# A fused attention, soft mixture of experts and feed-forward kernel: where tiles live, when weights are loaded, and dummy matmuls in the first units

## The chip, the cores and the metric

The kernel runs on one core of a Trainium2 chip. The metric is the time of one execution on the device in microseconds, as the median of some runs. A profile of one execution, taken by the hardware profiler, shows every instruction of the five engines: TensorE (PE; its weight loads are PEld), VectorE (DVE), ScalarE (ACT), GpSimd (POOL) and SyncE (SP), which here only issues transfers (DMAs).

## The reference

Three layers follow each other; all arrays are in float32, but `w_in` and `w_out` of the last layer come as 64-bit floats.

```python
# 1: attention with decay; B, H, S, D = 4, 8, 768, 48
for t in range(S):
    cur = einsum('bhd,bhe->bhde', u[None] * k_t, v_t)
    y[:, :, t] = einsum('bhd,bhde->bhe', r_t, state + cur)
    state = w[None, :, :, None] * state + einsum('bhd,bhe->bhde', k_t, v_t)
x = y.transpose(0, 2, 1, 3).reshape(3072, 384)
# 2: soft mixture of experts: 8 experts with 4 slots each
logits = x @ phi                                # 3072 x 32
slot_input = softmax(logits, over tokens).T @ x
slot_out[e] = relu(slot_input[e] @ w1[e]) @ w2[e]   # 384 -> 1024 -> 384
x = softmax(logits, over slots) @ slot_out
# 3: feed-forward
r = relu(x @ w_in); out = (r * r) @ w_out       # 384 -> 2048 -> 384
```

## The kernel before

The order of all work is written out by hand: each engine runs its instructions in the order of the code, and the framework only adds the waits. Transfers are issued by SyncE in the order of the code too, so a load that waits for its room holds up those behind it.

**Attention** goes in 16 units (`n`), four for each of the four batches; a unit is one batch and two heads, cut into six chunks of 128 tokens, in two groups of three. Each unit's inputs (r and k transposed in `tr`, and k, r and v in `krv`) are loaded into one of four unit slots; unit n+4 is loaded once unit n has been used. The steps of a unit, with their engines: `bonus` (GpSimd, two multiplications of the `krv` part, lines 237 and 238), `weigh` (VectorE, L242), `keys` (GpSimd, L248), `decay` (VectorE, L232, for k and for r), `diag` (GpSimd, L254, one for each group), `A` (TensorE, L264), `strict` (VectorE, L270, copies A's result onto diag's tile and so frees A's two banks), `KV` (TensorE, L278), `scan` (VectorE, L283, with a copy on ScalarE, L285), `Y` (TensorE, L301 and L307), `X` (L320, transposes the result into the tile of tokens xn) and `L` (L335, the logits). The loop at L440 interleaves units n-1, n and n+1; in it, `bonus(n+2)` is called at the end of turn n, `weigh(n+1)` and `keys(n+1)` at the start of turn n, and `KV(n+1)` in its middle. Two tiles xn take turns, for even and odd batches. `keep_clock(m)` issues m dummy matmuls of 128x256 on TensorE (L225), each of two instructions, into a bank that nobody reads. Before the first unit there are six.

**Weights.** `load_weight(i)` loads the next of 16 pieces of 1536 KB: the eight `w1[e]`, then the eight `w2[e]`. Nine have slots of their own and are loaded in the loop, one in each of the turns 0, 2, 3, 5, 6, 8, 9, 10 and 11, behind that turn's unit loads. The next three go into unit slots 0, 1 and 3 when their last units are done (turns 12, 13 and 15), and `load_win(0)` into unit slot 2. Two more (post0, post1) go where attention's tiles lay; that pool is closed as a whole after the last batch's sum over tokens (`soft_sum`, L378), at L528. The last two go into slots of w1 pieces after `up(1)` and `up(2)`.

**Experts.** `up(e)` (L564) and `down(e)` (L582) are TensorE's; `turn` transposes between them. `load_wout(f)` loads 128 rows of w_out (three buffers), and `wout_f32`, `conv_win` turn the 64-bit words into float32 in three steps on VectorE (L127, L129, L131). `wout_high` and `wout_low` split a piece of w_out in two parts. Before, three loads of w_out stand behind `up(3)`, and the parts 1 to 3 of w_in behind `up(4)` to `up(6)`; the conversions of w_out's pieces 0 to 2 and of w_in's parts 4 and 5 stand between the `down`s. Then follow `cstack` (L596, four transposes of the softmax over slots, with a copy on ScalarE, L597), the copy `so` of the outputs (L664), their transpose (L668, L671), and `G` (L677) with its split on ScalarE and VectorE (L681, L682).

**Feed-forward.** 96 turns in a loop (L774), each with one matmul of `s_h` (L725) and nine of the second product (L817) on TensorE; ScalarE and VectorE make relu, square and the split between them. In the turns 3, 11 and 19 `quarters` (L696) makes four more parts of G from w_in.

## Time and profile before

| | us |
|---|---|
| median of three runs (400.8 to 401.72) | 401.37 |
| the profiled execution, its own time | 400.18 |
| span of the profiled execution | 398.5 |
| TensorE busy in it | 381.7 |
| VectorE busy | 280.2 |
| ScalarE busy | 211.7 |
| GpSimd busy | 114.8 |

The transfers read 64.78 MB and write 4.72 MB. Attention lasts until about 129 us, the experts until about 158, the feed-forward loop from about 167 until the end.

How to read the rows: a stretch of the table of windows gives each engine's busy time in it with the number of instructions (x), the granted clock of TensorE as a share of 2.4 GHz, the mean share of the 16 transfer engines that was busy, and GB/s. A line of the timeline gives start, duration, engine, line of the kernel, operation, tiles (out<-in), and in brackets how long the engine was idle just before and what ended that. Instructions of the same kind that follow each other are one line (x); its duration reaches from the first start to the last end, and a matmul's end contains its drain. A busy TensorE is not TensorE at its peak.

### The profile page before, as it was taken

What the parts mean: (1) busy time and instruction counts of PE and PEld (TensorE: products, weight loads), DVE (VectorE), ACT (ScalarE), POOL (GpSimd) and SP (SyncE); (2) the same over time, 40 slices, a digit from 0 to 9 for tenths busy, and PEclk for the clock granted to TensorE, in tenths of its full rate; (3) what the DMA queues carried; (4) which work ended last, traced back from release to release, by engine and by line L of the source; (5) the groups of instructions that cost most, each with busy time, mean ns of one, the idle gap of its engine ahead of it and who ended that gap; (6) DMA issues with size and microseconds to landing.
All of it is one profiled execution on the core that took longest, in us unless ns stands there. A gap on an engine that the chain in (4) does not pass through costs nothing.

```text
span 398.5 us, 8194 instructions
## 1 busy us (share of the span) xinstructions
PE 381.7 (96%) x3219; PEld 294.2 (74%) x3219; DVE 280.2 (70%) x495; ACT 211.7 (53%) x465; POOL 114.8 (29%) x110
## 2 busy tenths in 40 slices
PE   5799999999999999789999999999999999999995
PEld 3677777767766564668787888888888888888884
DVE  5769897879974564799998567666566676566563
ACT  2224453453444451678888876555554564554552
POOL 3869997986870001122323120000000000000000
PEclk8559999999999999999999999999999999999999
DMA  7999999999995899913333202100000040000004
GB/s 245 344 320 343 389 407 403 404 404 406 405 383 188 307 410 405 375 47 102 85 100 87 63 0 104 56 0 2 0 0 2 0 159 2 0 0 2 0 0 158
DMA packets 25989, 70.81 MB, mean 178 GB/s; under 512 B 3680, under 2 KB 6112, under 8 KB 25952
## 3 DMA queue, kind: packets, MB, share of 16 engines
q1 hardware_dynamic: 25808, 70.10, 47.2%
q10 hardware_dynamic: 144, 0.20, 0.5%
q8 instruction: 25, 0.41, 0.4%
q14 instruction: 12, 0.10, 0.1%
HBM read 64.78 MB, written 4.72 MB: 174 GB/s over the span
## 4 chain that ended last, share of the span: by engine, by line
PE 80%; DMA 9%; DVE 6%; POOL 2%; issue 1%; ACT 1%; SPq 0%; POOLq 0%; ACTq 0%; DVEq 0%
PE ps_Y L817 16%; PE ps_A L817 16%; PE ps_kv L817 8%; PE ps_lg L817 8%; PE ps_A L264 7%; DMA wo<-in_w_out_dram 7%; PE ps_Y L307 5%; PE ps_Y L301 3%; PE ps_tr L320 3%; PE ps_tr L725 3%; PE ps_tab L725 3%; PE ps_lg L335 2%; DMA slot<-in_krv_dram 2%; PE ps_kv L278 2%; PE ps_tr L378 1%
## 5 line engine op out<-in xcount | busy, mean ns | idle before, releaser
L817 PE MATMUL ps_Y<-slot,slot 128*128 128x512 f32 x288 | 111.7, 395 | 0.0
L750 DVE TENSOR_TENSOR slot<-gg,slot 128x512 fp32r<-128x512 f32 (+1 forms) x97 | 66.5, 685 | 49.2 <-ACT slot L747 48.3
L817 PE MATMUL ps_A<-slot,slot 128*128 128x512 f32 x288 | 88.9, 393 | 0.6 <-DVE slot L682 0.6
L747 ACT CAST slot<-gg 128x512 fp32r<-128x512 f32 (+1 forms) x97 | 59.8, 618 | 50.5 <-DVE gg L744 49.9
L817 PEld LDWEIGHTS ps_A<-slot,slot 128*128 128x128 f32 x288 | 54.0, 188 | 13.2 <-DVE slot L682 1.0
L817 PEld LDWEIGHTS ps_Y<-slot,slot 128*128 128x128 f32 x288 | 54.1, 188 | 12.6 <-issue 0.6
L744 DVE TENSOR_TENSOR gg<-hr 128x512 f32<-128x512 f32 (+1 forms) x71 | 49.0, 691 | 14.3 <-ACT hr L737 14.2
L817 PE MATMUL ps_kv<-slot,slot 128*128 128x512 f32 x144 | 55.7, 394 | 0.0
L817 PE MATMUL ps_lg<-slot,slot 128*128 128x512 f32 x144 | 55.4, 391 | 0.0
L623 POOL TENSOR_TENSOR slot<-wf,slot 128x384 fp32r<-128x384 f32 x16 | 19.1, 1196 | 97.5 <-ACT slot L618 97.5
L270 DVE COPY_PREDICATED AT<-mask,ps_A 128x384 f32<-128x384 int32 x64 | 33.8, 583 | 9.2 <-PE ps_A L264 8.4
L264 PE MATMUL ps_A<-slot 48*128 48x128 f32 x384 | 36.2, 310 | 2.9 <-DVE slot L232 1.8
L264 PEld LDWEIGHTS ps_A<-slot 48*128 48x128 f32 x384 | 28.7, 204 | 10.3 <-DVE AT L270 3.6
L737 ACT ACTIVATE hr<-ps_tab 128x512 f32<-128x512 f32 x48 | 28.7, 599 | 12.9 <-PE ps_tab L725 12.9
L737 ACT ACTIVATE hr<-ps_tr 128x512 f32<-128x512 f32 (+1 forms) x49 | 28.8, 590 | 12.4 <-PE ps_tr L725 12.4
L313 ACT COPY xT<-ps_Y 112x256 f32<-112x256 f32 x64 | 17.4, 324 | 28.0 <-PE ps_Y L307 27.8
L254 POOL TENSOR_SCALAR_AFFINE_SELECT AT<-dg 128x768 f32<-128x768 f32 x32 | 28.0, 886 | 13.2 <-PE ps_Y L307 8.4
L817 PEld LDWEIGHTS ps_kv<-slot,slot 128*128 128x128 f32 x144 | 27.1, 188 | 6.2
L817 PEld LDWEIGHTS ps_lg<-slot,slot 128*128 128x128 f32 x144 | 27.0, 188 | 5.9
L232 DVE TENSOR_TENSOR slot<-slot,ps_tab 112x768 f32<-112x768 f32 x32 | 30.1, 941 | 0.6 <-DMA slot<-in_tr_dram 0.6
L307 PE MATMUL ps_Y<-AT,slot 128*48 128x128 f32 x384 | 29.6, 293 | 0.0
L307 PEld LDWEIGHTS ps_Y<-AT,slot 128*48 128x48 f32 x384 | 20.8, 129 | 6.5 <-issue 5.9
(168 smaller groups left out, 502.3 us busy)
## 6 DMA issues: line engine op xcount, KB each, us to landing
slot<-in_w_dram SPq DMA_DIRECT2D x14, 1536.0 KB, 11.1
slot<-in_tr_dram SPq DMA_DIRECT2D x32, 384.0 KB, 7.5
slot<-in_krv_dram SPq DMA_DIRECT2D x16, 448.0 KB, 7.3
slot<-in_krv_dram SPq DMA_DIRECT2D x16, 416.0 KB, 7.8
slot<-in_w_in_dram SPq DMA_DIRECT2D x4, 1536.0 KB, 19.1
wo<-in_w_out_dram SPq DMA_DIRECT2D x16, 384.0 KB, 3.3
out_dram<-os SPq DMA_DIRECT2D x15, 256.0 KB, 2.2
post<-in_w_dram SPq DMA_DIRECT2D x2, 1536.0 KB, 9.2
```

The source lines that it names most:

```text
L232: nc.vector.tensor_tensor(x, x, t.unsqueeze(1).to_broadcast([112, NC, 128]), ALU.mult)
L254: nc.gpsimd.affine_select(out=at.rearrange("p c h t -> p (c h) t"), in_=dg.rearrange("p c h -> p (c h)").unsqueeze(2).to_broadcast([128, 2 ...
L264: nc.tensor.matmul(p[h][:, i], tv[rows, 1, GC * g + i], tv[rows, 0, GC * g + i], start=True, stop=True)
L270: nc.vector.copy_predicated(at[:, :, h], mask.unsqueeze(1).to_broadcast([128, GC, 128]), p[h])
L307: nc.tensor.matmul(at_of(c, j), vv[:, c, h], at[:, c - GC * g, h], start=False, stop=True, skip_group_check=True)
L623: nc.gpsimd.tensor_tensor(wout_half(wls, f, WL), st.pop(("wf", f)), hi, ALU.subtract)
L725: nc.tensor.matmul(p, gst[:, 128 * f:128 * (f + 1)], cTall[:, 512 * g:512 * (g + 1)], start=True, stop=True)
L737: nc.scalar.activation(fs[i, "hr"][:, c], fs[i, "p"][:, c], AF.Relu)
L744: nc.vector.tensor_mul(gg, hr, hr)
L747: nc.scalar.copy(part(i, "gh")[:, c], fs[i, "gg"][:, c])
L750: nc.vector.tensor_tensor(part(i, "gl")[:, c], fs[i, "gg"][:, c], fs[i, "gh"].bitcast(F32)[:, c], ALU.subtract)
L817: nc.tensor.matmul(o, (hi, lo, hi)[k][:, 128 * j:128 * (j + 1)], (gh, gh, gl)[k], start=(f == 0 and k == 0), stop=(f == NF - 1 and k == 2))
```

## The change

1. Attention's short-lived tiles no longer lie in one pool. Three rooms (`yards`, `odd`, `even`) hold views of them: `yards` the three tiles of diag, the two of scan's copies and the table P; `odd` and `even` the two tiles xn, and `odd` also `pkn` and scan's result. Each room is given on as one, when all its views have been read: `even` to the three buffers of w_out's loads (after the third batch's sum), `yards` to the weight piece 12 (after the last Y), `odd` to the piece 13 (after the last sum). In the feed-forward loop the rings of `hr`, `gg` and `os` lie in `yards` and `odd`.
2. The first two weight pieces are loaded before the loop, ahead of unit 4; in the loop the turns 0, 2, 4, 6, 8, 10 and 11 load one.
3. Three loads of w_out are issued in turn 14; the parts 1 to 3 of w_in come behind all weights, two more w_out loads behind the first of them. Pieces 0 and 1 of w_out are converted ahead of the last batch's softmax, piece 2 at `down(3)`, and the parts 4 to 7 of w_in at `down(4)` to `down(7)`.
4. The outputs' copy `so` goes ahead of the first `cstack`; the third `cstack` goes into turn 16 of the loop.
5. 16 dummy matmuls instead of 6 before the first unit, and 14 more in groups of 4, 3, 3 and 4 around A, Y and KV of unit 0.

```diff
+    ROOM = {"yards": 3072, "odd": 3072, "even": 2310}
+
+    def room(tag, dt=F32):
+        cnt[0] += 1
+        return const.tile([128, ROOM[tag]], dt, name=f"{tag}{cnt[0]}", tag=tag, bufs=1)
...
     load_n(0)
+    yards, odd, even = (room(t) for t in ROOM)
+    att = att_cm.__enter__()
...
     def load_wout(f):
-        wst["o", f] = wk([128, DM, 2], "wo", NWO, I32, pool=mid)
+        if "wo" not in wst:
+            wst["wo"] = room("even", I32)
+        wst["o", f] = wst["wo"][:, 2 * DM * (f % NWO):2 * DM * (f % NWO + 1)].rearrange("p (d t) -> p d t", t=2)
...
-    home = list(range(NB, NSLOT)) + [0, 1, 3, "post0", "post1", NB + 1, NB + 2]
+    home = list(range(NB, NSLOT)) + [0, 1, 3, "yards", "odd", NB + 1, NB + 2]
...
-    SB = [att.tile([112, NC, D], F32, name=f"SB{i}") for i in range(2)]
-    pkn = att.tile([128, NP, 2, D], F32, name="pkn")
-    xn = [att.tile([128, NC, DM + 1], F32, name=f"xn{i}") for i in range(2)]
+    o = 3 * 2 * GC * 128
+    ATS = [yards[:, o // 3 * i:o // 3 * (i + 1)].rearrange("p (c h t) -> p c h t", c=GC, h=2) for i in range(3)]
+    SB = [yards[:112, o + NC * D * i:o + NC * D * (i + 1)].rearrange("p (c d) -> p c d", c=NC) for i in range(2)]
+    o = NC * (DM + 1)
+    xn = [x[:, :o].rearrange("p (c d) -> p c d", c=NC) for x in (even, odd)]
+    pkn = odd[:, o:o + DM].rearrange("p (a b d) -> p a b d", a=NP, b=2)
+    sc = odd[:112, o + DM:o + DM + D * NC].rearrange("p (d c) -> p d c", c=NC)
...
+        if i == 2 and 2 <= f < NF - NWO:
+            load_wout(f + NWO)
...
-    keep_clock(6)
+    keep_clock(16)
...
+    keep_clock(4)
     A(0, 0)
+    keep_clock(3)
...
-    nload = 0
+    for nload in range(2):
+        load_weight(nload)
+    nload = 2
     for n in range(NU):
...
+        if n == 0:
+            keep_clock(3)
         Y(n, 0)
+        if n == 0:
+            keep_clock(4)
...
-            if n not in (1, 4, 7):
+            if n not in (1, 3, 5, 7, 9):
                 load_weight(nload)
                 nload += 1
         elif n == NU - 2:
+            for f in range(NWO):
+                load_wout(f)
             load_win(0)
...
+    load_weight(nload)
+    nload += 1
 
     L(NU - 1, (1, 2))
     keep_clock(1)
+    for f in range(2):
+        for i in range(3):
+            wout_f32(f, i)
     soft_max(B - 1)
...
-    while str(home[nload]).startswith("post"):
-        load_weight(nload)
-        nload += 1
+    load_weight(nload)
+    nload += 1
...
-        if e == 3:
-            for f in range(NWO):
-                load_wout(f)
         if e in (4, 5, 6):
             load_win(e - 3)
+        if e == 4:
+            load_wout(NWO)
+            load_wout(NWO + 1)
...
-    hT = take(WIN[1])[:, :256 * E].rearrange("p (i e j f) -> p i e j f", i=E // 2, e=2, j=2)
+    hT = take(CT)[:, :256 * E].rearrange("p (i e j f) -> p i e j f", i=E // 2, e=2, j=2)
...
         down(e)
-        if e < 3:
+        if e in (1, 3):
+            wout_high(e // 2)
+            wout_low(e // 2)
+        if e == 3:
             for i in range(3):
-                wout_f32(e, i)
-            if e < 2:
-                wout_high(e)
-                wout_low(e)
-        elif e < 5:
-            conv_win(e + 1)
-    cstack(0, "lg")
+                wout_f32(2, i)
+        if e >= 4:
+            conv_win(e)
+    cTall = take(CT, F32R)
...
     nc.scalar.copy(so, acc[:, :DM])
+    cstack(0, "lg")
     cstack(1, "kv")
...
-    cstack(2, "lg")
     G(0, "A")
...
-    todo = [(f, i) for f in range(6, NF) for i in range(3)]
+    todo = [(f, i) for f in range(8, NF) for i in range(3)]
...
-        for _ in range(2 if i < 3 else 2 - half):
+        for _ in range(2 if i < 5 else 1):
...
-        if i in (22, 25, 28):
-            cstack(3 + (i - 20) // 3, ("tr", "tab")[(i + 1) % 2])
+        if i in (16, 22, 25, 28):
+            cstack(2 if i == 16 else 3 + (i - 20) // 3, ("tr", "tab")[(i + 1) % 2])
```

## Rows read from the trace of the kernel before

**Rows 1.** The page: busy tenths of TensorE and granted clock, in 40 slices of the span.

```profile
PE   5799999999999999789999999999999999999995
...
PEclk8559999999999999999999999999999999999999
```

**Rows 2.** Windows: stretch, length, five engines busy (PE, PEld, DVE, ACT, POOL), clock, DMA share, GB/s.

```profile
5.78:8.57 2.79, 0.00 (x1) 0.00 (x1) 2.51 (x14) 0.71 (x2) 0.06 (x1) 0.88 1.03 410
...
20.00:28.00 8.00, 8.00 (x69) 6.17 (x71) 5.22 (x8) 1.63 (x5) 5.46 (x5) 0.50 0.89 324
...
17.00:24.00 7.00, 6.56 (x68) 5.10 (x68) 5.74 (x9) 1.17 (x3) 6.77 (x7) 0.50 0.94 336
24.00:31.00 7.00, 7.00 (x92) 5.57 (x92) 3.33 (x7) 2.31 (x9) 3.95 (x5) 0.69 0.86 300
...
50.00:113.00 63.00, 62.16 (x998) 46.31 (x988) 54.38 (x93) 28.82 (x101) 53.52 (x46) 1.00 1.03 405
...
117.00:134.00 17.00, 15.87 (x200) 9.96 (x195) 6.80 (x20) 7.46 (x26) 0.81 (x1) 1.00 0.72 262
```

**Rows 3.** Timeline of the first units, TensorE and GpSimd.

```profile
1.43 4.36 PE L225 MATMUL ps_tr<-ident 128*128 128x256 f32 x12 [1.43 <-POOL ident masks.py:199]
...
4.97 0.81 PE L225 MATMUL ps_tr<-ident 128*128 128x256 f32 x3
...
11.33 1.65 PE L264 MATMUL ps_A<-slot 48*128 48x128 f32 x12 [1.75 <-DVE slot L232]
...
18.86 1.04 PE L278 MATMUL ps_kv<-slot 128*48 128x48 f32 x20 [0.44 <-POOL slot L248]
...
28.29 0.67 PE L278 MATMUL ps_kv<-slot 128*48 128x48 f32 x20
...
28.58 0.87 POOL L254 TENSOR_SCALAR_AFFINE_SELECT AT<-dg 128x768 f32<-128x768 f32 x1 [2.97 <-PE ps_Y L307]
```

**Rows 4.** Unit 3's last load: its issue (timeline), and its time to landing (DMA view).

```profile
16.59 0.43 SPq L92 DMA_DIRECT2D slot<-in_tr_dram  x1
...
slot<-in_tr_dram SPq DMA_DIRECT2D x1, 384.0 KB, 7.8
```

**Rows 5.** Timeline at units 4 and 5.

```profile
36.00 1.41 POOL L237 TENSOR_TENSOR slot<-slot,U 128x576 f32<-128x576 f32 x1
...
42.22 1.41 POOL L237 TENSOR_TENSOR slot<-slot,U 128x576 f32<-128x576 f32 x1
...
45.20 1.42 POOL L248 TENSOR_TENSOR slot<-slot,pkn 128x576 f32<-128x576 f32 x1
...
46.69 1.06 DVE L270 COPY_PREDICATED AT<-mask,ps_A 128x384 f32<-128x384 int32 x2
47.28 0.62 PE L278 MATMUL ps_kv<-slot 128*48 128x48 f32 x20
...
48.40 0.94 PE L264 MATMUL ps_A<-slot 48*128 48x128 f32 x12
```

**Rows 6.** Timeline at the last softmax over tokens.

```profile
129.30 0.42 DVE L343 TENSOR_REDUCE nmx<-ps_lg 96x1 f32<-96x256 f32 x1 [5.17 <-PE ps_lg L335]
```

**Rows 7.** Timeline from `down` to the first quarters.

```profile
154.28 0.36 DVE L127 TENSOR_SCALAR wf<-wo 128x384 int32<-128x384 int32 x1 [8.34 <-DMA wo<-in_w_out_dram]
...
154.67 0.56 DVE L129 SCALAR_TENSOR_TENSOR wf<-wo,wf 128x384 int32<-128x384 int32 x1
...
158.77 0.60 PE L596 MATMUL ps_kv<-ident,cs 128*128 128x128 f32 x4
...
159.99 0.94 PE L668 MATMUL ps_tr<-sel,so 128*128 128x128 f32 x6 [0.62 <-ACT so L664]
...
162.46 0.27 ACT L681 CAST slot<-ps_A 128x128 fp32r<-128x128 f32 x1 [0.48 <-PE ps_A L677]
...
163.24 0.29 DVE L682 TENSOR_TENSOR slot<-ps_A,slot 64x128 fp32r<-64x128 f32 x1
...
176.20 0.84 PE L696 MATMUL ps_tr<-slot,soT 128*32 128x128 f32 x18 [1.15 <-DVE slot L131]
```

More of the change, by code (lines that the diff above doesn't have):

```diff
@@ L163, in load_weight @@
         kind, e = W[i]
-        if str(home[i]).startswith("post"):
-            cnt[0] += 1
-            t = post.tile([128, 3072], F32, name=f"post_{cnt[0]}", tag=home[i], bufs=1)
-        else:
-            t = take(home[i])
+        t = (room if home[i] in ROOM else take)(home[i])
         if kind == "w1":
@@ L190, in rwkv_softmoe_ffn @@
     pw = att.tile([112, 2, 8], F32, name="pw")
-    P = att.tile([112, 2 * NP, 64], F32, name="P")
+    P = yards[:112, 2 * 2 * GC * 128:2 * 2 * GC * 128 + 2 * NP * 64].rearrange("p (a n) -> p a n", n=64)
     nc.vector.memset(P[:, :NP, 0:1], 1.0)
@@ L403, in slots_norm, with wout_half, wout_f32, wout_high @@
         nc.vector.tensor_mul(cnat[:, b], cnat[:, b], sm.unsqueeze(2).to_broadcast([128, NC, NS]))
+    whs, wls = {}, {}
+    def wout_half(half, f, homes):
+        if f // 8 not in half:
+            half[f // 8] = take(homes[f // 8], F32R).rearrange("p (c d) -> p c d", c=8)
+        return half[f // 8][:, f % 8]
+    def wout_f32(f, i):
+        if f >= NF:
+            return
+        if i == 0:
+            st["wf", f] = wk([128, DM], "wf", 2)
+        to_f32(st["wf", f], wst["o", f], (i,))
+        if i == 2 and 2 <= f < NF - NWO:
+            load_wout(f + NWO)
+    def wout_high(f):
+        if 0 <= f < NF:
+            nc.scalar.copy(wout_half(whs, f, WH), st["wf", f])
+    def wout_low(f):
+        if 0 <= f < NF:
+            hi = wout_half(whs, f, WH).bitcast(F32)
+            nc.gpsimd.tensor_tensor(wout_half(wls, f, WL), st.pop(("wf", f)), hi, ALU.subtract)
     P2 = const.tile([96, 2, DM + 1], F32, name="P2")
@@ L597, in cstack @@
         nc.scalar.copy(cTall[:, 512 * g:512 * (g + 1)], p)
-    whs, wls = {}, {}
-    def wout_half(half, f, homes):
-        if f // 8 not in half:
-            half[f // 8] = take(homes[f // 8], F32R).rearrange("p (c d) -> p c d", c=8)
-        return half[f // 8][:, f % 8]
-    def wout_f32(f, i):
-        if f >= NF:
-            return
-        if i == 0:
-            st["wf", f] = wk([128, DM], "wf", 2, pool=mid)
-        to_f32(st["wf", f], wst["o", f], (i,))
-        if i == 2 and f + NWO < NF:
-            load_wout(f + NWO)
-    def wout_high(f):
-        if 0 <= f < NF:
-            nc.scalar.copy(wout_half(whs, f, WH), st["wf", f])
-    def wout_low(f):
-        if 0 <= f < NF:
-            hi = wout_half(whs, f, WH).bitcast(F32)
-            nc.gpsimd.tensor_tensor(wout_half(wls, f, WL), st.pop(("wf", f)), hi, ALU.subtract)
     soft_turn(B - 1, slice(1, 2))
@@ L661, in rwkv_softmoe_ffn @@
     parts = take(PARTS, F32R).rearrange("p (i r c) -> p i r c", i=2, r=3)
+    yards, odd = room("yards"), room("odd")
+    rings = {"hr": [yards[:, 512 * i:512 * (i + 1)] for i in (0, 1)], "gg": [yards[:, 512 * i:512 * (i + 1)] for i in (2, 3)],
+             "os": [r[:, 512 * i:512 * (i + 1)] for r, i in ((yards, 4), (yards, 5), (odd, 0), (odd, 1))]}
+    nos = 0
     so = wk([128, DM], "so", 1, pool=ffn)
     nc.scalar.copy(so, acc[:, :DM])
+    cstack(0, "lg")
     cstack(1, "kv")
@@ L725, in s_h @@
         nc.tensor.matmul(p, gst[:, 128 * f:128 * (f + 1)], cTall[:, 512 * g:512 * (g + 1)], start=True, stop=True)
-        fs[i, "p"], fs[i, "hr"] = p, wk([128, 512], "hr", 2, pool=ffn)
-        fs[i, "gg"] = wk([128, 512], "gg", 2, pool=ffn)
+        fs[i, "p"], fs[i, "hr"], fs[i, "gg"] = p, rings["hr"][i % 2], rings["gg"][i % 2]
     def part(i, tag):
@@ L820, in rwkv_softmoe_ffn @@
                 tok = 512 * (2 * sg + half)
-                os = wk([128, 512], "os", 4, pool=ffn)
+                os = rings["os"][nos % 4]
+                nos += 1
                 for e in range(2):
```

5 lines of the change are left out of this document (1 added, 4 removed).

## The prediction

> **What bounds the kernel now.** I read the slices of the page first. TensorE is busy in tenths 9 from about 20 us to the end, in attention and in the feed-forward part alike, so the sum is one of TensorE's time: a microsecond counts only if it comes off TensorE's queue, a gap in it, or its clock [rows 1]. The slices show a granted clock of 0.5 (1.2 GHz, against 2.4) in three slices near the start, and the stretch 20 to 28 us in the table has 0.50 with TensorE busy all of it [rows 1, 2]. Six dummy matmuls ended near 5.8 us, TensorE then had nothing for 2.79 us while the decay tables were made, and the clock fell and stayed low through the real work of units 0 and 1 [rows 2, 3]. Second, the transfers: from 50 to 113 us they run at 405 GB/s with a share of 1.03, full; from 17 to 31 us at 300 to 336, and from 117 to 134 at a share of 0.72, so there is room early and late, but none between [rows 2]. Third, the gaps between the last `down` and the feed-forward loop, in the timeline [rows 7]. GpSimd is the engine to watch beside TensorE: a unit costs it two bonus steps, keys and two diags, 3 x 1.42 + 2 x 0.87 = 6.0 us, against 6.2 from one bonus to the next (36.00, 42.22) [rows 3, 5].
>
> **Dummy matmuls in the first units.** Ten more ahead of the decay tables, 14 more between the real steps of unit 0. Three dummy instructions at the high clock took 0.81 us including their drain; a dummy is two of them, so at most 0.54, and by their spacing 0.43 [rows 3]. Sixteen in a row end near 1.43 + 4.36 + 10 x 0.43 = 10.1 us, 1.5 past the start of the table transposes, which is hidden because the first A waits for VectorE until 11.33 [rows 3]. With the 4, 3, 3 and 4 more, and the real steps at about half their duration (KV 1.04 against 0.62, A 1.65 against 0.94), A(0,0) ends at 12.9, as before; KV(1) starts at 20.0, not at 18.86, where it waited for GpSimd; and KV(2) at 25.3 instead of 28.29 [rows 3, 5]. There GpSimd takes over: its diag that idled 2.97 us for TensorE until 28.58 no longer waits [rows 3]. So units 2 and 3 run **3.0 us** earlier, if their inputs are there.
>
> **Two weights before the loop.** This is where that gain goes. SyncE's loads share one queue, and the two weights are put between unit 3's loads and unit 4's. Unit 3's last load was issued at 16.59 and landed 7.8 later, at 24.4 [rows 4]. A weight is 384 x 1024 floats, 1.573 MB; a unit is 128 x (2 x 768 + 1728) floats, 1.671 MB. At 405 GB/s behind 24.4 us, two weights and unit 4 are 4.82 MB, 11.9 us, so unit 4 is in at 36.3 us; one more weight, which the loop issues behind it, and unit 5 make 8.0, so 44.3 [rows 2, 4]. Before, unit 4's bonus started at 36.00 and unit 5's at 42.22 [rows 5]. The slack behind a late bonus: keys(5) ended at 45.20 + 1.42 = 46.62 and TensorE's KV(5) began at 47.28, 0.66 us; and on VectorE weigh(5) and decay(5,1), which wait for unit 5, stand ahead of strict(4,1), which freed A's two banks at 47.75 for A(5,0) at 48.40, 0.65 us [rows 5]. So unit 4 lets attention be at most 0.4 earlier than before (36.3 - 36.00 - 0.7), whatever the clock does, and unit 5 makes it 44.3 - 42.22 - 0.65 = **1.4 us later**. From there TensorE has no gaps in which to make it up [rows 1]. Bounds: if the transfer engines' spare time between 17 and 24 us (69 GB/s under 405, 0.48 MB) takes the weights in early, 1.2 less, +0.2; if the 300 GB/s of 24 to 31 us holds although more is queued, 1.7 more, +3.1 [rows 2]. I take the middle, since the queue behind these loads is then as deep as at 50 us. Later units don't bind: every second unit of the loop brings no weight, and two units with one weight are 4.92 MB, 12.1 us, against 12.4 of compute.
>
> **Weights and w_out earlier.** Two pieces of w2 and three of w_out get room that attention gives up early, inside the stretch with a share of 0.72 [rows 2]. This is no gain by itself: the gaps that TensorE has behind attention are waits for other engines, not for a weight. On SyncE's queue the w_out loads wait for the third batch's sum to have read the even x tile; behind them stand w_in's first load, which could go only when unit 14 is done, and the fourth w2 piece. They buy this: w_out's words no longer arrive at 154.28, after VectorE had sat idle 8.34 us for them, and w_in's second part no longer queues behind three w_out loads (1.18 MB, 2.9 us) [rows 7]. The two w_out conversions that move ahead of the last softmax are 2 x (0.36 + 0.56 + 0.56) = 3.0 us on VectorE, where it was idle for 5.17 us; with w_out late there, up to 3.0 would land on the softmax chain [rows 6, 7].
>
> **Outputs copied first.** ScalarE's copy of the outputs goes ahead of the first stack's copy, to right behind `down`. TensorE's eight transposes, the second four of which began at 158.77, still hold the next matmul to about 159.2 instead of 159.99: **0.8 us** [rows 7]. Further on, ScalarE's split copy ended at 162.46 + 0.27 = 162.73, but VectorE took its half at 163.24, behind six conversion steps of w_in; these are now done before, another **0.5** [rows 7]. Together the feed-forward's first matmul comes 1.3 us sooner after `down`, or 0.8 if VectorE is still late. The wait of 1.15 us at 176.20, for conversions of w_in's parts 6 and 7, goes: **1.15** [rows 7]. The third stack's four transposes were free, inside the wait for the outputs' transpose, and now stand in the full loop; four such take 0.60 with their drain, so I charge **0.45**, between 0 and 0.6 [rows 7]. The rings and the new views add no instruction, and VectorE's work in the loop only shrinks.
>
> **Sum.** +1.4 - 1.3 - 1.15 + 0.45 = -0.6, with bounds of -2.2 (0.2 - 1.3 - 1.15) and +1.8 (3.1 - 0.8 - 1.15 + 0.6). The profiled execution has a span of 398.5 and a time of 400.18, so 397.9 and 399.6 there; the median of the runs shown is 401.37, 1.2 above it, so **400.8**.
>
> **Rivals.** (1) *The clock falls while TensorE waits for unit 4.* This one ends slower. KV(4), one unit before 47.28, so 41.1, would come 3.0 early, at 38.1, and waits for keys(4), 4.4 behind the bonus, until 40.7: 2.6 us idle; and 1.9 one unit later [rows 5]. After the 2.79 us at the start the clock was down; from 117 to 134, where 1.1 us were idle in pieces, it stayed at 1.00; 2.6 lies between [rows 2]. Against it: by the lower bound of the transfers the first wait is only 1.4 us. At 1.2 GHz the way from KV(1) to KV(2) took 28.29 - 18.86 = 9.4 us instead of 6.2, and TensorE was so busy for the whole of it before the clock rose [rows 1, 3]: +3.2 to +4.5 on the -0.4, or on the +1.4 if it falls in the second wait, so some +3 to +5.5 in attention and 403.5 in all (402.2 to 405). It decides if the 2.6 us come in one piece and are enough. The Trainium skill has this as a rule (TensorE: Matmul & The Clock Gate, "HAM oscillation — how this bites in real kernels"): matmul bursts with DMA waits between them fall back to the low clock; the fall at the start of this trace agrees. (2) *The inputs don't bind.* If transfers between 17 and 44 us do better than the full rate, or GpSimd's lateness is taken up elsewhere, attention keeps 1 to 3 us: 401.4 - 2 - 2 = 397.4 (396.4 to 398.4). Against it: a load lands no sooner than the queue ahead of it. (3) *The dummies don't hold the clock.* At the low clock a dummy is twice 0.43, and the 14 in unit 0 are 12 us, of which some 7 show: 406.5. Against it: six of them raised it, and the new ones leave no idle piece.
>
> **Chances.** Forecast 0.40 (own range 399.2 to 403.2), clock falls 0.33, inputs don't bind 0.20, dummies fail 0.07. A difference under 0.2%, 0.8 us, can't be told from none with this kernel, so faster means under 400.6 and slower above 402.2. Of the forecast a third is faster and a twentieth slower; rival 2 is all faster; rivals 1 and 3 are slower but for a tenth: faster 0.34, same 0.28, slower 0.38. The range 397.8 to 404.8 leaves out half of rival 2, the end of rival 1, and rival 3.
>
> **What would show it.** Clock: 1.00 in every stretch from 8 to 35 us; a stretch of 0.5 behind 38 us is rival 1. Gate: GpSimd's bonus for units 4 and 5 waits for in_krv and starts near 36.3 and 44.3, and KV(5) near 48.7. Behind `down`: the output copy at its end, the split subtraction without six conversions ahead of it, no wait at the first quarters, four more transposes in the loop. The forecast is wrong if bonus(5) starts before 42.9, or if TensorE waits for a weight in `down`.

## The result, and the profile after

The changed kernel took 405.27 us against 401.40 us of the kernel before (medians of 20 executions each). The two medians alone have a ratio of 1.0096; the ratio of the whole measurement, which leaves out one execution of the changed kernel that counts as slow (408.75 us), is 1.0081, with a 95% interval of 1.0057 to 1.0106. The kernel became slower, where the forecast was 400.8 us, and 405.27 lies 0.5 us above the end of the stated range as well. What came is the first rival: the clock fell while TensorE waited for unit 4. A slower feed-forward loop, which no part of the prediction has, came on top.

The executions of the changed kernel show it without a profile: in twelve of the 20 the mean granted clock was 0.981 to 0.987 and the median time 406.6 us, in the other eight it was 0.993 or more and the median 402.5 us. So the fall costs some 4.1 us where it comes, and without it the change still gives 1.1 us away. (Two of the eight, at 0.993 and 403.7 us, lie between; whether they had a shorter fall isn't seen, since they have no profile.) The profiled execution has the fall (time 407.12, span 405.4, against a span of 398.5 before).

From the page of the changed kernel, TensorE's busy tenths and the granted clock, in 40 slices of the span, to be read against [rows 1]:

```profile
PE   8998899999999899899999999999999999999995
...
PEclk9999579999999999999999999999999999999999
```

The slow clock of the first slices is gone; instead slices 5 and 6, some 41 to 61 us, have it. The windows of the changed kernel, cut at those places (columns as in [rows 2]: stretch, length, five engines busy, clock, DMA share, GB/s):

```profile
8.00:38.00 30.00, 30.00 (x401) 23.34 (x401) 22.96 (x36) 9.71 (x29) 22.11 (x22) 1.00 1.02 384
38.68:42.23 3.55, 0.00 (x1) 0.01 (x1) 1.31 (x2) 0.54 (x2) 3.39 (x4) 0.97 1.03 402
42.23:55.50 13.27, 13.27 (x140) 10.11 (x142) 7.23 (x12) 2.94 (x10) 8.37 (x8) 0.50 1.02 400
55.80:62.00 6.20, 6.20 (x111) 4.87 (x110) 5.48 (x9) 2.66 (x12) 4.79 (x5) 1.00 0.67 226
```

From 8 to 38 us TensorE is busy all the time at 2.4 GHz, where before the granted clock was 0.50 from 17 to 24 us and 0.69 from 24 to 31 [rows 2]. Then it does nothing for 3.55 us, the clock goes to 1.2 GHz at the end of that, and the next 13.27 us bring only 140 matmuls; 6.2 us at the high clock bring 111.

What it waited for stands in the timelines of GpSimd and TensorE, to be read against [rows 5]:

```profile
26.79 1.42 POOL L248 TENSOR_TENSOR slot<-slot,U 128x576 f32<-128x576 f32 x1
...
38.01 1.40 POOL L248 TENSOR_TENSOR slot<-slot,U 128x576 f32<-128x576 f32 x1 [4.61 <-DMA slot<-in_krv_dram]
...
40.96 1.21 POOL L259 TENSOR_TENSOR slot<-slot,odd 128x576 f32<-128x576 f32 x1
...
42.23 1.04 PE L289 MATMUL ps_kv<-slot 128*48 128x48 f32 x20 [3.55 <-POOL slot L259]
...
45.93 1.42 POOL L248 TENSOR_TENSOR slot<-slot,U 128x576 f32<-128x576 f32 x1 [2.13 <-DMA slot<-in_krv_dram]
```

L248 is the bonus, L259 keys, L289 KV. The bonus of unit 3 starts at 26.79; that of unit 4 only at 38.01, since its last load has landed then, and GpSimd was idle for 4.61 us for it. Keys(4) ends at 42.17, and KV(4) follows. Unit 5 is late as well, at 45.93 (before: 36.00 and 42.22 [rows 5]).

Where the 6.9 us of the two spans came from, by the start of some matmuls (us):

| TensorE starts | before | after | step |
|---|---|---|---|
| first `up` | 135.42 | 142.29 | attention +6.87 |
| last matmul of `down` | 157.86 | 164.72 | 0.0 |
| first product of the loop, 1st | 163.59 | 169.09 | -1.36 |
| 7th | 179.18 | 183.46 | -1.22 |
| 22nd | 214.73 | 219.77 | +0.76 |
| 34th | 244.77 | 250.11 | +0.30 |
| 96th, the last | 387.48 | 394.28 | +1.46 |
| end of the span | 398.46 | 405.38 | +0.12 |

The part between `down` and the loop gives the 2.6 us that it should. Attention takes 6.9, and the loop, whose work the change hardly touches, 2.6 more. The lines behind the gain, from the timelines of ScalarE, VectorE and TensorE after, against [rows 7]:

```profile
165.33 0.48 ACT L693 COPY so<-ps_Y 128x384 f32<-128x384 f32 x1 [8.16 <-PE ps_Y L632]
...
168.74 0.29 DVE L712 TENSOR_TENSOR slot<-ps_A,slot 64x128 fp32r<-64x128 f32 x1 [0.35 <-ACT slot L711]
...
183.46 0.50 PE L755 MATMUL ps_tr<-slot,slot 128*128 128x512 f32 x1 [0.16 <-DVE gq L735]
```

The outputs' copy (L693) starts with the end of `down`; VectorE's split (L712) is idle 0.35 us for ScalarE's half, where before it came behind six conversions; and the wait of 1.15 us at the first quarters [rows 7] is one of 0.16.

And the loop's pace: from the 34th first product to the 96th there are 620 matmuls. Before (timeline, TensorE, the line of the first product):

```profile
244.77 0.40 PE L725 MATMUL ps_tab<-slot,slot 128*128 128x512 f32 x1
...
387.48 0.40 PE L725 MATMUL ps_tab<-slot,slot 128*128 128x512 f32 x1
```

After:

```profile
250.11 0.39 PE L755 MATMUL ps_tab<-slot,slot 128*128 128x512 f32 x1
...
394.28 0.39 PE L755 MATMUL ps_tab<-slot,slot 128*128 128x512 f32 x1
```

142.71 us before, 230.2 ns from one matmul to the next; 144.17 after, 232.5 ns. Nothing in the prediction accounts for that.

### The profile page after: what moved, and what is told of

Read it like the earlier page. It is cut to its first block, busy times and chain, and to the rows that moved or that the text cites. A ratio compares the mean times of both kernels' runs of the same rounds, so it can differ in the third digit from the quotient of the medians.

```text
span 405.4 us, 8296 instructions
## 1 busy us (share of the span) xinstructions
PE 392.1 (97%) x3267; PEld 300.8 (74%) x3267; DVE 279.3 (69%) x495; ACT 213.0 (53%) x465; POOL 111.3 (27%) x110
## 4 chain that ended last, share of the span: by engine, by line
PE 87%; DMA 4%; DVE 4%; ACT 2%; issue 1%; POOL 1%; SPq 0%; ACTq 0%; POOLq 0%; DVEq 0%
PE ps_A L845 16%; PE ps_Y L845 16%; PE ps_lg L845 8%; PE ps_kv L845 8%; PE ps_A L275 6%; PE ps_Y L317 5%; PE ps_tr L236 4%; DMA slot<-in_krv_dram 4%; PE ps_Y L311 3%; PE ps_tr L330 3%; PE ps_tr L755 3%; PE ps_Y L632 3%; PE ps_A L614 3%; PE ps_tab L755 3%; PE ps_lg L345 2%; PE ps_kv L289 2%
## 5 line engine op out<-in xcount | busy, mean ns | idle before, releaser
L779 DVE TENSOR_TENSOR slot<-yards,slot 128x512 fp32r<-128x512 f32 (+1 forms) x97 | 66.5, 686 | 52.7 <-ACT slot L776 51.9
L776 ACT CAST slot<-yards 128x512 fp32r<-128x512 f32 (+1 forms) x97 | 59.9, 618 | 50.2 <-DVE yards L773 49.6
L773 DVE TENSOR_TENSOR yards<-yards 128x512 f32<-128x512 f32 (+1 forms) x71 | 48.9, 690 | 16.3 <-ACT yards L766 16.2
L281 DVE COPY_PREDICATED yards<-mask,ps_A 128x384 f32<-128x384 int32 x64 | 33.9, 584 | 9.4 <-PE ps_A L275 8.5
L766 ACT ACTIVATE yards<-ps_tab 128x512 f32<-128x512 f32 x48 | 28.7, 599 | 13.8 <-PE ps_tab L755 13.7
L766 ACT ACTIVATE yards<-ps_tr 128x512 f32<-128x512 f32 (+1 forms) x49 | 28.8, 589 | 12.2 <-PE ps_tr L755 12.2
L275 PE MATMUL ps_A<-slot 48*128 48x128 f32 x384 | 34.4, 301 | 0.5 <-DVE yards L281 0.4
L265 POOL TENSOR_SCALAR_AFFINE_SELECT yards<-dg 128x768 f32<-128x768 f32 x32 | 28.0, 886 | 16.4 <-PE ps_Y L317 9.4
L317 PE MATMUL ps_Y<-yards,slot 128*48 128x128 f32 x384 | 28.9, 288 | 0.0
L248 POOL TENSOR_TENSOR slot<-slot,U 128x576 f32<-128x576 f32 x16 | 22.6, 1411 | 12.2 <-DMA slot<-in_krv_dram 12.2
## 6 DMA issues: line engine op xcount, KB each, us to landing
slot<-in_w_dram SPq DMA_DIRECT2D x14, 1536.0 KB, 10.2
```

The source lines that it names most:

```text
L248: nc.gpsimd.tensor_tensor(rv, rv, U[:, n % NP].unsqueeze(1).to_broadcast([128, NC, 2, D]), ALU.mult)
L265: nc.gpsimd.affine_select(out=at.rearrange("p c h t -> p (c h) t"), in_=dg.rearrange("p c h -> p (c h)").unsqueeze(2).to_broadcast([128, 2 ...
L275: nc.tensor.matmul(p[h][:, i], tv[rows, 1, GC * g + i], tv[rows, 0, GC * g + i], start=True, stop=True)
L281: nc.vector.copy_predicated(at[:, :, h], mask.unsqueeze(1).to_broadcast([128, GC, 128]), p[h])
L317: nc.tensor.matmul(at_of(c, j), vv[:, c, h], at[:, c - GC * g, h], start=False, stop=True, skip_group_check=True)
L766: nc.scalar.activation(fs[i, "hr"][:, c], fs[i, "p"][:, c], AF.Relu)
```

## Experiments: the dummies and the early weights apart

The theory after the result: the dummies bring 2.7 to 3 us, the early weights make units 4 and 5 late, and only the two together make TensorE wait long enough for the clock to fall. The rival: one of the two costs the time by itself, or the rooms do.

**dum_late**, the changed kernel with the weights' loads of the loop as before, none ahead of unit 4:

```diff
-    for nload in range(2):
-        load_weight(nload)
-    nload = 2
+    nload = 0
...
-            if n not in (1, 3, 5, 7, 9):
+            if n not in (1, 4, 7):
```

> The changed kernel with the weight loads of the loop as before (turns 0, 2, 3, 5, 6, 8 to 11, none ahead of unit 4); the dummies stay. Theory (the early weights make units 4 and 5 late, TensorE waits in one piece, and the wait takes its clock): no wait of GpSimd for in_krv at units 4 and 5, KV(4) near 38.2, clock 1.00 from 8 us on; the next gate is unit 8, so attention ends 0.5 to 2 us earlier than before, and with 2 us saved behind it about 398.5 us (397.5 to 399.7). Rival A (attention's matmuls are too light to hold the clock once the dummies end): the clock falls near 40 us here too, 402 to 405. Rival B (the merged rooms add waits or slow the loop): no fall, but 401 or more.

Measured: 397.76 us, 0.9929 (0.9906 to 0.9951) of the kernel before. Its windows:

```profile
8.00:38.00 30.00, 30.00 (x401) 23.35 (x401) 25.37 (x42) 10.19 (x30) 26.57 (x26) 1.00 1.00 366
38.00:62.00 24.00, 24.00 (x407) 17.97 (x403) 18.96 (x32) 11.52 (x37) 21.06 (x19) 1.00 1.02 396
```

TensorE has no wait and a clock of 1.00 through units 1 to 7; the bonus of unit 4 starts at 33.33 and KV(4) at 38.5, against 41.1 before. The first `up` starts at 131.7, 3.7 us sooner than before. The change without its early weights is faster.

**nodum_early**, the changed kernel without the new dummies:

```diff
-    keep_clock(16)
+    keep_clock(6)
...
-    keep_clock(4)
     A(0, 0)
-    keep_clock(3)
...
-        if n == 0:
-            keep_clock(3)
         Y(n, 0)
-        if n == 0:
-            keep_clock(4)
```

> The changed kernel with the dummies of before (six, none in unit 0); the two early weights stay. Theory: clock 0.5 until about 28 us as before, units 4 and 5 in at 37.9 and 45.9 as in the changed kernel, TensorE's two waits only about 1.2 and 1.9 us since it comes 3 us later, so the clock stays up; attention 3.1 later than before, minus 2 behind it: 402.5 us (401.5 to 403.5). Rival A: the same here, since it has no lead to lose. If the clock falls in these shorter waits as well: 405 or more.

Measured: 402.49 us, 1.0046 (1.0018 to 1.0074). In the profiled execution the clock is low from 10.7 to 31.2 us, as it was before, and 1.00 from there to the last matmuls. One of the twelve executions took 407.65 us at a mean clock of 0.956, against 0.968 to 0.974 in the others; it has no profile. From its timelines of GpSimd and TensorE:

```profile
44.54 1.42 POOL L248 TENSOR_TENSOR slot<-slot,U 128x576 f32<-128x576 f32 x1 [1.15 <-DMA slot<-in_krv_dram]
...
48.78 0.43 PE L289 MATMUL ps_kv<-slot 128*48 128x48 f32 x10 [0.17 <-POOL slot L259]
```

The last loads of units 4 and 5 landed at 36.5 and 44.5 us, near the 36.3 and 44.3 of the forecast and 1.4 us sooner than in the profiled execution of the changed kernel. TensorE, without the new dummies, comes to KV(4) only at 42.28, when even the later landing would have been in time, so it idles 0.17 us ahead of KV(5) instead of 3.55 ahead of KV(4). KV(5) starts at 48.78 (before: 47.28 [rows 5]), and the first `up` is 1.54 us later than before.

**nodum_late** undoes both parts; the rooms, the moved loads and conversions and the earlier copy of the outputs stay. Its edit is the two diffs above together.

> The changed kernel with the dummies and the loop's weight loads of before: what is left is the rooms, the moved w_out and w_in loads and conversions, and the outputs' copy. Theory: attention as before to 0.3 us, 2 us less behind it (1.4 at the outputs, 1.1 at the quarters, 0.5 back for the third stack): 399.4 us (398.8 to 400.2). Rival B: 401 or more, with attention or the loop slower than before in the profile.

Measured: 400.49 us, 0.9999 (0.9972 to 1.0026). A miss by 1.1 us: the gain behind `down` is there (5.73 us from the last `down` to the first product before, 4.37 here), but attention is 0.8 us longer, and the loop, from the 34th first product to the 96th, 0.9. On the base of the changed kernel, then, in us:

| | early weights | weights as before |
|---|---|---|
| new dummies | 405.27 | 397.76 |
| six dummies | 402.49 | 400.49 |

The dummies win 2.7 us without the early weights and lose 2.8 with them. (405.27 was measured beside a kernel before of 401.40 us, the other three beside one of 401.02.)

**before_dum**, the kernel before with the new dummies and nothing else:

```diff
-    keep_clock(6)
+    keep_clock(16)
...
+    keep_clock(4)
     A(0, 0)
+    keep_clock(3)
...
+        if n == 0:
+            keep_clock(3)
         Y(n, 0)
+        if n == 0:
+            keep_clock(4)
```

> The kernel before with the dummies alone (16 instead of 6 at the start, 4, 3, 3 and 4 more in unit 0). Theory (the prediction's first step): the clock stays at 1.0 through units 1 to 5, units 2 and 3 come 3.0 us earlier, unit 4 (landed 30.5 in the kernel before) is in time, and the later units keep the gain: 398.4 us (397.5-399.5). Rival (the gain is lost at later inputs, or needs the other parts): 400.5 to 401.4.

Measured: 398.54 us, 0.9947 (0.9921 to 0.9973), as expected. Its profiled execution (401.49) is one of two of the twelve that took over 401; the profile says why. Timelines of GpSimd and TensorE:

```profile
61.03 1.41 POOL L237 TENSOR_TENSOR slot<-slot,U 128x576 f32<-128x576 f32 x1 [1.77 <-DMA slot<-in_krv_dram]
...
68.14 1.40 PE L264 MATMUL ps_A<-slot 48*128 48x128 f32 x12 [1.10 <-DVE AT L270]
```

And a window of it:

```profile
70.80:77.50 6.70, 6.70 (x74) 5.33 (x73) 3.64 (x6) 1.54 (x6) 4.10 (x5) 0.50 1.03 405
```

Being some 2 us earlier uses up the lead of the inputs further on too: here GpSimd waits 1.77 us for unit 8, TensorE idles 1.10 ahead of its next A, and 2.6 us after that wait the clock is low for 6.8 us. A gain at the start can make a later input that was just in time a late one.

## Experiments: the wait and the clock

**hold** is the changed kernel with dummies in the two places where it waits, so that TensorE stays busy while the inputs come late as they do:

```diff
+        if n in (3, 4):
+            keep_clock(7 if n == 3 else 5)
```

> The changed kernel, and seven more dummies ahead of KV(4) and five ahead of KV(5), so that TensorE has work while it waits for units 4 and 5. Theory: units 4 and 5 as late as in the changed kernel, clock 1.00 throughout attention, so only the late inputs are left: attention 3.1 later than before, minus 2 behind it, 402.5 us (401.8 to 403.5), and the spread between runs goes. Rival A: the clock falls later all the same, 405.

Measured: 404.37 us, 1.0091 (1.006 to 1.0123). Windows of its profiled execution (403.22):

```profile
38.50:42.00 3.50, 3.50 (x26) 2.83 (x26) 1.92 (x3) 0.54 (x2) 3.34 (x4) 1.00 1.03 403
42.00:56.00 14.00, 14.00 (x210) 10.61 (x208) 9.94 (x17) 4.58 (x15) 10.69 (x11) 1.00 1.03 404
```

TensorE's timeline there:

```profile
38.53 3.29 PE L236 MATMUL ps_tr<-ident 128*128 128x256 f32 x14
41.75 0.65 PE L289 MATMUL ps_kv<-slot 128*48 128x48 f32 x20
```

The bonus of unit 4 starts at 37.16, 0.85 us sooner than in the changed kernel, but keys(4) still end at 41.34, 2.8 us after TensorE would have begun to idle. The dummies fill the wait, the clock is 1.00 from 42 to 56 us, where the changed kernel had 0.50, and 14 us bring 210 matmuls. None of the six executions has the mean clock of 0.981 to 0.987 of the changed kernel's falls. So it is the idle TensorE, not the late unit as such, that lowers the clock. As a price for the late inputs alone hold is no good measure: KV(5) starts at 50.4, 1.6 later than in nodum_early, with five dummies ahead of it, and three of its six executions have a mean clock of 0.993 and over 405 us, for which there is no profile. That was my mistake in the experiment, and its time came out 2 us above what was expected.

**early_sparse** keeps the two early weights, but puts none behind the loads of units 4, 5 and 6, so that unit 4 alone is late:

```diff
-            if n not in (1, 3, 5, 7, 9):
+            if n not in (0, 1, 2, 4, 7):
```

> The changed kernel with its two early weights, but with no weight behind the loads of units 4, 5 and 6 (weights behind those of units 7, 9, 10 and so on). Unit 4 should land as late as in the changed kernel (37.9, bonus 38.0, KV(4) at 42.2 after a wait of 3.55 us), unit 5 about 4 us earlier than there (near 42 instead of 45.9), so the second wait goes. Theory (the wait for unit 4 alone makes the clock fall): 0.5 from about 42 for some 13 us in part of the runs, 402 to 405 us in those, near 400.5 in runs without a fall. Rival (it takes both waits, units 4 and 5): the clock stays at 1.0 in all runs, and the time is near 400.5: dum_late's 397.8 plus the late unit 4, 42.2 less 38.5, less what the later units give back.

Measured: 400.04 us, 0.9998 (0.9965 to 1.0032); four of twelve executions took 403.9 to 406.1 at a mean clock of 0.982 to 0.990, the other eight 399.5 to 401.6 at 0.997 or more. The profiled one (404.93) is one of the four. Unit 4 landed at 36.9, a microsecond sooner than in the changed kernel, and GpSimd did not wait for unit 5. TensorE's timeline:

```profile
41.30 0.66 PE L289 MATMUL ps_kv<-slot 128*48 128x48 f32 x20 [2.44 <-POOL slot L259]
```

And the windows of the wait and of what came after it:

```profile
38.86:41.30 2.44, 0.01 (x1) 0.00 (x0) 1.30 (x2) 0.54 (x2) 2.36 (x3) 1.00 1.02 399
42.50:52.50 10.00, 10.00 (x97) 7.88 (x94) 5.18 (x9) 2.60 (x9) 5.75 (x6) 0.50 0.72 250
```

One wait of 2.44 us is enough, in a third of the executions: the first theory holds. What decides between two executions of the same kernel isn't seen here.

**one_early** has one weight ahead of unit 4's loads, and the other eight as in dum_late:

```diff
-    nload = 0
+    load_weight(0)
+    nload = 1
...
-            if n not in (1, 4, 7):
+            if n not in (0, 1, 4, 7):
```

> dum_late with one weight (W0) moved from behind unit 4's loads to ahead of them; the dummies stay, the other eight weights stay where dum_late has them. In dum_late unit 4's last load landed at 29.54 us and unit 5's at 38.92; a weight's load takes the queue 3.8 to 4.2 us. Theory (an input costs only what it is later than its turn): unit 4 lands near 33.7, its bonus starts there, KV(4) needs 4.2 us after that, 37.9, which is before its turn at 38.5; unit 5 is as before. Nothing waits, the clock stays at 1.0: 397.8 us (397-399). Rival (any weight ahead of unit 4 delays the unit by its own 3.8 us, or lets the clock fall): KV(4) at 40 or later and 400 us or more.

Measured: 398.02 us, 0.9918 (0.9893 to 0.9942), the same as dum_late. Unit 4's last load landed at 33.04, 3.5 us later than in dum_late, but its bonus had its turn only at 34.40, and KV(4), at 39.5, waited for nothing; the clock was 1.00. From the timelines of GpSimd and TensorE:

```profile
34.40 1.41 POOL L248 TENSOR_TENSOR slot<-slot,U 128x576 f32<-128x576 f32 x1
...
39.53 0.62 PE L289 MATMUL ps_kv<-slot 128*48 128x48 f32 x20
```

No idle time stands in brackets behind either. (KV(4) is 1 us later than in dum_late because in this execution the units run 1 us later from KV(0) on.) One weight fits in the lead that unit 4 has, two don't.

## Experiments: the pace of the loop

The rest is the loop: 230.2 ns from matmul to matmul before, 231.7 in dum_late and nodum_late, 232.5 in the changed kernel, hold and nodum_early, each the same to 0.1 in kernels with the same order of tiles, on different chips. So it goes with something that is fixed when the kernel is built. The new order of requests moves tiles to other addresses: the slots, in the order of their first use, lie behind each other, with small tiles between them. The slots themselves can't shift anything modulo 256 bytes (13,056 bytes of a unit slot are 51 x 256, 12,288 of the others 48 x 256), but the new room `even`, of 9,240 bytes, can, and so can the tiles `sel`, `rm` and `ones`, of 576 bytes with their padding, which come ahead of slot 5 when weights are late and behind slot 6 when two are early. (The addresses here and below are those that the built programs give the tiles.) What TensorE reads in the loop: w_out's parts as weights, from the slots 12 and 1 for the first eight blocks of 128 columns, and from 5 and 6 for the others; and the squares' parts as the moving operand, from slot 2.

**late_pad**, dum_late with an unused tile ahead of the rooms:

```diff
+    const.tile([128, 8], F32, name="pad")
     yards, odd, even = (room(t) for t in ROOM)
```

> dum_late with an unused tile of 32 bytes per partition ahead of the three rooms, which moves the rooms, the weights' slots 4 to 12 and the attention's tiles up by 32 bytes. In the kernel before these tiles start at multiples of 64 bytes, in the changed one 32 bytes beside them. Theory (a tile's address sets the matmul's pace in the loop): the mean from matmul to matmul after 245 us goes from 231.7 ns back to 230.1, as in the kernel before: 1.0 us of 640 matmuls; and the 0.8 us by which nodum_late's attention was longer than that of the kernel before goes too: 396.0 us. Rival (the pace comes of other engines' order): 231.7 ns and 397.8 us.

Measured: 393.74 us, 0.9825 (0.9793 to 0.9856). 32 unused bytes give 4 us; the pace is 226.7 ns, and it hardly varies any more (226 or 227 ns between all matmuls from the 35th first product to the 96th, where one in ten was so short in dum_late and most had 229 to 236). The theory that the address matters holds, and gave more than was expected of it: from the 7th first product to the end the profiled execution took 216.9 us instead of 221.3. Attention didn't get shorter, against the expectation: the first `up` started at 133.70 in the profiled execution, 2.0 us later than in dum_late's, which was its fastest.

**late_slots** has the same tile behind the rooms, so that they stay, and **late_pad96** has 96 bytes instead of 32 in late_pad's place:

```diff
     yards, odd, even = (room(t) for t in ROOM)
+    const.tile([128, 8], F32, name="pad")
```

```diff
+    const.tile([128, 24], F32, name="pad")
     yards, odd, even = (room(t) for t in ROOM)
```

> dum_late with the unused 32 bytes behind the rooms instead of ahead of them: the rooms stay where dum_late has them, the slots 5, 6 and 12, which hold w_out's halves as the loop's stationary operand, start at multiples of 128 bytes as in late_pad (each weight tile of 128 columns is 512 bytes of a row). Theory (the address of the stationary operand sets the loop's pace): 226.7 ns from matmul to matmul after 245 us, as in late_pad, and 393.8 us (393-395). Rival (the rooms' address does it, where the squares are written): 231.7 ns and 397.8 us.

> dum_late with an unused tile of 96 bytes instead of 32 in late_pad's place: the rooms go to multiples of 128 bytes, the slots 5, 6 and 12 to 64 bytes beside one, as they are in the kernel before. Theory (the stationary operand wants multiples of 128): 230.1 ns from matmul to matmul, as in the kernel before, and some 396.2 us. Rival (multiples of 64 do, or the rooms): 226.7 ns and 393.8 us.

Measured: late_slots 393.59 us, 0.9794 (0.9763 to 0.9824), 226.7 ns; late_pad96 399.19 us, 0.9943 (0.9916 to 0.997), 233.0 ns. It isn't the rooms, and with all tiles at multiples of 64 bytes (late_pad96) the loop is slower than without (dum_late). The two rows of late_slots:

```profile
240.41 0.39 PE L754 MATMUL ps_tab<-slot,slot 128*128 128x512 f32 x1
...
380.94 0.39 PE L754 MATMUL ps_tab<-slot,slot 128*128 128x512 f32 x1
```

140.53 us for 620 matmuls.

**before_pad** does it to the kernel before, and **after_align** to the changed one:

```diff
             nc.gpsimd.memset(ones, 1.0)
+            const.tile([128, 16], F32, name="pad")
```

```diff
     yards, odd, even = (room(t) for t in ROOM)
+    const.tile([128, 24], F32, name="pad0")
...
             nc.gpsimd.memset(ones, 1.0)
+            const.tile([128, 16], F32, name="pad1")
```

> The kernel before with an unused tile of 64 bytes behind the tile of ones, so that the slots 5, 6 and 12 move from 64 bytes beside a multiple of 128 to one; nothing else of it changes. Theory: 226.7 ns instead of 230.1 from matmul to matmul; from the seventh first product to the end 216.9 us (late_pad) instead of 219.3: 398.6 us (398-399.5). Rival (the pace belongs to the new rooms): 230.1 ns and 401 us.

> The changed kernel whole, early weights and all, with unused tiles of 96 and 64 bytes that bring the slots 5, 6 and 12 to multiples of 128 bytes. Theory: 226.7 ns instead of 232.6 from matmul to matmul, some 4.9 us less from the seventh first product to the end (221.9 before the edit, 216.9 in late_pad), and the wait for unit 4 with its clock fall as before: near 397.5 us in runs without a fall, 401.5 in those with one. Rival (the pace came of the early weights' order itself): 232.6 ns and 405 us.

Measured: before_pad 398.26 us, 0.9926 (0.9893 to 0.9958), 226.7 ns, so that the pace is no matter of the rooms or of the change: the kernel before had it too, and was 3 us from what 64 bytes make of it. after_align 403.57 us, 1.0059 (1.0036 to 1.0082), a miss: 227.5 ns where the weights come from the slots 5 and 6, but 233.3 ns where they come from 12 and 1, although 12 is at a multiple of 128 now. So a multiple of 128 isn't the rule either. Its profiled execution shows something on the clock besides: unit 4 landed at 36.8 us, TensorE idled 1.43 us ahead of KV(4) and 1.37 ahead of KV(5), at 49.04, and from 51.0 to 61.2 us the clock was 0.50; all eleven executions have a mean clock of 0.983 to 0.987.

Here are the addresses modulo 256 and the paces of these kernels side by side (the squares lie at 128). A pace is the mean of 160 matmuls: for the blocks of columns 1 to 8 from the 35th first product to the 51st, for the others from there to the 67th.

| kernels | slot 12 | blocks 1 to 8 | slots 5, 6 | blocks 9 to 16 |
|---|---|---|---|---|
| late_pad, late_slots, before_pad | 128 | 226.7 ns | 128, 128 | 226.7 ns |
| after_align | 0 | 233.3 | 128, 128 | 227.5 |
| before | 64 | 230.3 | 64, 64 | 230.0 |
| dum_late | 96 | 231.4 | 96, 96 | 232.0 |
| after | 96 | 231.3 | 32, 32 | 233.8 |
| late_pad96 | 192 | 232.6 | 192, 192 | 233.4 |

Slot 1 is at 128 in all. The fast cases are those in which the weights lie where the squares do, modulo 256. Two readings are left: that address as such, or the distance between the two operands. **after_align2** brings slot 12 there as well in the changed kernel, **all_shift** moves all of late_slots by 128 bytes, and **parts_shift** moves the squares' parts of late_slots alone by 128 bytes:

```diff
-            const.tile([128, 16], F32, name="pad1")
+            const.tile([128, 112], F32, name="pad1")
```

```diff
+    const.tile([128, 32], F32, name="pad0")
     units = [take(i, cols=SLOT[i]) for i in range(NB)]
```

```diff
-    parts = take(PARTS, F32R).rearrange("p (i r c) -> p i r c", i=2, r=3)
+    parts = take(PARTS, F32R, cols=3104)[:, 32:].rearrange("p (i r c) -> p i r c", i=2, r=3)
```

> after_align with the second unused tile 448 bytes instead of 64, so that slot 12 too begins at 384 modulo 512 bytes, like the slots 1, 5 and 6. Theory (the pace needs both halves of w_out at the same place modulo 512 bytes): 226.7 ns from matmul to matmul in all of the loop, 216.9 us from the seventh first product to the end (after_align: 220.0), and about 400.5 us, still with the wait for unit 4 and the clock fall. Rival (the early weights' order itself slows the first eight blocks of the FFN's columns): 233 ns there as in after_align, 403.6 us.

> late_slots with 128 unused bytes ahead of all tiles, so that everything moves together: w_out's halves begin at 0 modulo 512, the squares' parts (the moving operand) at 256 instead of 128. Theory (the distances between the operands count): 226.7 ns and 393.6 us as in late_slots. Rival (the absolute address counts, 384 modulo 512): 230 to 234 ns and 396.5 us or more.

> late_slots with the squares' parts, the moving operand of the second product, 128 bytes later in their slot (256 instead of 128 modulo 512); w_out's halves stay at 384. If the distance from the weights to the moving operand counts: over 230 ns from matmul to matmul and 396 us or more. If only where the weights lie counts: 226.7 ns and 393.6 us.

Measured: after_align2 400.15 us, 0.9982 (0.9959 to 1.0005), 226.7 ns in all of the loop; all_shift 392.83 us, 0.9814 (0.9765 to 0.9863), 226.7 ns; parts_shift 397.56 us, 0.9913 (0.9879 to 0.9948), 231.3 ns. The rows of parts_shift, against those of late_slots:

```profile
240.45 0.39 PE L754 MATMUL ps_tab<-slot,slot 128*128 128x512 f32 x1
...
383.88 0.39 PE L754 MATMUL ps_tab<-slot,slot 128*128 128x512 f32 x1
```

143.43 us instead of 140.53, with the weights where they were. It is the distance: the weights moved alone (after_align to after_align2) and the squares moved alone (parts_shift) change the pace, both moved together (all_shift) don't. In all kernels with 226.7 ns throughout, the stationary and the moving operand are 256 bytes apart modulo 512; at each of the other distances tried a matmul follows the one before after 230 to 234 ns. A distance of 0 modulo 512 was in no run, so that any multiple of 256 would do is not shown. after_align2 is the changed kernel with nothing but its tiles set right; it still has the wait and the fall (clock 0.983 to 0.987 in all twelve executions) and is level with the kernel before. all_shift and late_slots are the best kernels of this study: the change without its early weights, and with its tiles set right, takes 2% off the kernel before.

## Why the prediction was wrong, step by step

**Dummies: right.** The clock is 1.00 from 8 to 38 us in the changed kernel. KV(2) started at 25.7 (forecast 25.3, before 28.29). Worth 3.0 us by the prediction; 2.7 (dum_late against nodum_late) and 2.3 (before_dum) measured.

**Early weights: right as a price at a steady clock.** Forecast: units 4 and 5 in at 36.3 and 44.3, and attention 1.4 us later than before. They landed at 37.9 and 45.9. The weights were in at 32.3, where the sum at 405 GB/s puts them too (24.4 and 3.15 MB: 32.2); the last load of unit 4 took 2.5 us, when loads of its size take 1.05, and that is the difference. This is a matter of the execution: in the other kernels that have two early weights unit 4 landed at 36.5 (nodum_early), 36.8 (after_align), 36.9 (early_sparse), 37.0 (hold) and 37.1 us (after_align2). The price is confirmed by nodum_early, +1.54 in attention with units 4 and 5 in at 36.5 and 44.5; the eight executions of the changed kernel with a mean clock of 0.993 or more, 1.1 us slower than before, agree.

**Choice between forecast and first rival: wrong.** This is the step that failed. The rival put TensorE's wait at 2.6 us and the fall at +3 to +5.5 in attention, 403.5 in all (402.2 to 405). The wait was 3.55, with unit 4 later than forecast. The fall came in 12 of 20 executions, cost 4.1 us between the two groups, and in the profiled one attention is +6.9. The rival's mechanism was described as it came; I gave it 0.33 against 0.40 because of the lower bound of the transfers, by which the wait would have been only 1.4 us. The same prediction, though, took the middle of those bounds for the landing, and by the middle the wait was 2.6 us. early_sparse shows that 2.44 us suffice in some executions, so that the wait as forecast would have been enough. The sum itself let the landings alone set the length of attention and gave the wait of TensorE no price: the 3.0 us won by the dummies ahead of a fixed landing come back as a wait, less what slack there was, and that stood only in the rival. The time of the rival fell short too, since it also lacks the slower loop (below). The Trainium skill has a rule (TensorE: Matmul & The Clock Gate, "HAM oscillation — how this bites in real kernels"), that matmul bursts with DMA waits between them fall back to the low clock. The traces agree with it: 0.50 after the 3.55 us behind a late load in the changed kernel, and 1.00 in dum_late and one_early, which have no such wait.

**Behind `down`: right.** Forecast -1.3 for the outputs and the split, -1.15 for the quarters; measured -1.36 and -1.22. The third stack, +0.45: with the same pace in the loop, the way from the 7th first product to the 22nd takes 35.17 us in before_pad and 35.66 in after_align2, +0.49.

**Rings and views: mis-sized.** "The rings and the new views add no instruction" is true and was taken for "cost nothing". This is the second step that failed. The rooms moved the weights' slots against the squares' (231.7 ns a matmul in dum_late and nodum_late, 230.2 before), and the earlier requests of the weights moved them again (232.5 ns in the changed kernel); from the 7th first product to the end that is 219.28 us before and 221.92 after, +2.6, of which 0.5 is the stack. So 2.1 us were missing in the sum, a term put at nothing.

**The sum again.** 401.4 + 1.4 (attention, at a steady clock) - 2.6 + 0.5 (behind `down`, stack) + 2.1 (pace) = 402.8, where the executions without a fall have 402.5; with 4.1 for the fall 406.9, where the others have 406.6. The 4.1 is itself the difference of the two groups, so only the first of the two sums is a check.

**What stays open.** Why the clock falls in one execution and not in another of the same kernel. Why loads land 1 to 2 us later in one execution than in another: attention is 0.8 us longer in nodum_late than before, and 1.5 in before_pad, whose edit doesn't concern it, and in both the traces show unit 8's last load landing later (62.7 and 63.5 us, 61.4 before), GpSimd waiting for it (1.57 and 1.91 us) and then TensorE idle (0.91 and 1.01 us). And what in the chip makes the distance between operands count: only that it does is shown.

## What to carry over

A gain ahead of a transfer is worth only the lead that this transfer has; look up the landing of each later input, and add the wait that the gain opens, before adding gains. On TensorE such a wait of 2.4 to 3.6 us cost some 4 us more than its own length in a part of the executions, since the clock fell with it. And an edit that moves tiles is not free because it adds no instruction: compare the start-to-start time of the same matmuls before and after, and if it differs, the operands' addresses are a suspect that an unused tile of a few bytes can test.

## What the runs showed of the hardware that was not expected

The distance of a matmul's two operands in SBUF changed the pace of this loop. For its 128x512 matmuls, at a granted clock of 1.00, it was 226.7 ns with the weights and the moving operand 256 bytes apart modulo 512, and 230 to 234 ns with the weights of a block, or part of them, 32, 64, 96 or 128 bytes beside that. The same 128 bytes on both sides (all_shift) changed nothing, and on one side (parts_shift) cost 2.9 us of 620 matmuls. In the whole kernel that was 4 us of 398 (dum_late to late_pad), more than any part of the change brought by itself.

After a fall the clock stayed low for 13.7 us in the changed kernel, 10.2 in early_sparse and 6.8 in before_dum, with TensorE busy for nearly all of it; in after_align it was 10.2 us after two waits of 1.43 and 1.37. The shortest wait seen ahead of a fall was 1.10 us (before_dum); waits of 0.91 us (nodum_late) and 1.01 us (before_pad) had none behind them.
